# One order table for a whole kernel, weight loads per row chunk, 128-column kv weights and early query tiles

## The chip, the cores and the metric

The kernel runs on one core of one Trainium2 chip. The metric is the device time of one execution in microseconds; lower is better. A profile is one further view: it counts from the first to the last instruction, which is about 1.7 us less than the device time of the same execution. "PE" is TensorE, "DVE" VectorE, "ACT" ScalarE, "POOL" GpSimd, "SP" the engine that issues most DMAs, "PEld" the weight loads of PE.

## The reference

```python
# S=2048 tokens, D=640, H=32 heads of 20, F=1728; all bf16
x = A_x
g = sigmoid((x * gate_w).sum(-1, keepdims=True))
# a: linear attention
q, k, v = split_heads(x @ wqkv)                      # 2048 x 640 each
pq, pk = q @ w_phi, k @ w_phi                        # per head, 20 x 20
phi = lambda p: concat([softmax(p), softmax(-p)])    # 40 features a head
kv = einsum("bhsf,bhsd->bhfd", phi(pk), v)           # sums over all tokens
z  = phi(pk).sum(tokens)
a  = (phi(pq) @ kv) / (phi(pq) . z + 1e-6) @ wo
# b: gated FFN
b = (silu(x @ w_gate) * (x @ w_up)) @ w_down
return g * a + (1 - g) * b
```

## The kernel before

The program is straight-line: Python functions emit instructions, and a tracker puts semaphore waits between them. Work is cut into items: the transposes of a token tile of x (`xpose`), its values (`vtile`), its keys (`ktile`), its kv sums (`kvtile`), its queries (`qtile`), a gate-and-up item of the FFN (`fitem`: 10 matmuls of 512 columns), an attention output (`oitem`), a down projection (`ditem`). The order in which the items are emitted is the order on every engine. Before, that order came from numbers: each item was given a position on an axis, and the list was sorted.

```python
put(-20, xpose, 0); put(-20, gcol); put(-19, vhalf, 0, 0); put(-18.5, xpose, 1); ...
for m in range(5):
    put(-10 + 0.1 * m, premult, 1, m)                       # keys: wk times w_phi
    put((2.1, 3.1, 3.3, 3.4, 4.4)[m], premult, 0, m)        # queries: wq times w_phi
for t in range(NT):                                         # 16 token tiles of 128
    put(t, ktile, t); put(t + 3.6, kvtile, t)
    if t >= 6: put(t - 2.2, vtile, t)
put(NT + 2.7, kv_finish); put(NT + 4.2, z_broadcast)
...                                                         # fitem, qtile, oitem, ditem
```

The kv sums, and the query tile, whose VectorE work was emitted in two parts, one and two items after the exponentials:

```python
def kvtile(t):
    for j in range(NCH):                                    # 11 blocks of 3 heads x 40 features
        o = bank(bk, 63 * jj, 63 * jj + 63, 0, 120)
        pairs.append((o, ekr[:, b, 120 * j:120 * j + 120],  # weights: 120 columns
                      v1r[:, t % NV, 63 * j:63 * j + 63], ...))

def qtile(t):
    pr = tok_proj(t, 0); head_exps(pr, e)                   # PE, then two exponentials on ACT
    def vec_a():
        reduce(qz, e); tt("dve", ez, e, zb, mult)           # sums, numerators of the denominator
    def vec_b():
        reduce(qw, ez); ...                                 # small operations, then the scaling
        tt("pool", ph, eq, qc, mult); dma(phiT, ph, transpose=True)
    defer(1, vec_a); defer(2, vec_b)
```

The softmax here doesn't subtract the row's maximum and nothing guards it: scores larger than these inputs give would overflow.

Of the kernel before, what the change touches and what calls it, by code (L numbers as in the profile page):

```python
# [18 lines left out]
ACTF = mybir.ActivationFunctionType
# [5 lines left out]
BANK = 2048  # L25

# [144 lines left out]
def _build(nc, A_x, A_wqkv, A_w_phi, A_wo, B_x, B_w_gate, B_w_up, B_w_down, gate_w, out):  # L171
# [37 lines left out]
    qz = sb("qz", [P, 2, 64], F32)  # L209
# [7 lines left out]
    ekr = nc.alloc_sbuf_tensor_at("ekr", [P, 4, FP], BF16, offset=hbase + 14 * 512 * 2)  # L217
# [93 lines left out]
    def memset(e, a, v):  # L311
        eo = tr.eng[e]
        return run(e, lambda: eo.memset(a, v), [], [a])

    def dma(e, dst, src, transpose=False):
        eo = tr.eng[e]

        def fn():
            if transpose:
                return eo.dma_start_transpose(dst, src)  # L320
            return eo.dma_start(dst, src)
        rd = [src] if src.tensor.name in tr.base else []
        wr = [dst] if dst.tensor.name in tr.base else []
        return run(e, fn, rd, wr, dma=True)
# [16 lines left out]
    wv_src = A_wqkv[:, 2 * D:3 * D].rearrange("(c p) j -> p c j", p=P)  # L341
    wk_src = A_wqkv[:, D:2 * D].rearrange("(c p) j -> p c j", p=P)
# [3 lines left out]
    dma("sp", wvg[:, :, 0:320], wv_src[:, :, 0:320])  # L346
    load_x(1)
    dma("sp", wvg[:, :, 320:D], wv_src[:, :, 320:D])
    load_x(2)
    load_x(3)  # L350
    dma("sp", wkn[:, :, :], wk_src)
# [21 lines left out]
    v1v = v1r[:, :, :].rearrange("p b (h d) -> p b h d", d=DH + 1)  # L373
    memset("dve", v1v[:, :, H, :], 0.0)
    memset("dve", v1v[:, :, :, DH:DH + 1], 1.0)
    memset("dve", ekr[:, :, 1280:FP], 0.0)
    memset("dve", krec[:, :, :], 0.0)
    memset("pool", wog[:, :, :], 0.0)
    memset("pool", ones[:, :], 1.0)
# [24 lines left out]
    deferred = []  # L404

    def tick():
        for d in deferred:
            d[0] -= 1
        while deferred and deferred[0][0] <= 0:
            deferred.pop(0)[1]()  # L410

    def defer(n, fn):
        deferred.append([n, fn])
        deferred.sort(key=lambda d: d[0])

    ring = {"n": 3, "i": 0}
# [19 lines left out]
    vpr = {}  # L436

    def vhalf(t, hb):
        if t not in vpr:
            vpr[t] = next_pair()  # L440
        pr = vpr[t]
        n = 320 + hb
        mm(group(bank(2 * pr + hb, 0, n), [(xT[:, t, c, :], wvg[:, c, 320 * hb:320 * hb + n]) for c in range(5)]))
        if hb:
            i = halves(pr).rearrange("p b (h d) -> p b h d", d=DH)
            o = v1v[:, t % NV, 0:H, 0:DH].rearrange("p (b h) d -> p b h d", b=2)
            copy("act", o, i)
            copy("act", svec[:, t:t + 1], bank(2 * pr + 1, 320, 321))

    def vtile(t):  # L450
        vhalf(t, 0)
        vhalf(t, 1)
# [31 lines left out]
    def kvtile(t):  # L484
        b = t % 4
        pairs = []
        for j in range(NCH):
            bk, jj = (KV0, j) if j < 8 else (KV0 + 1, j - 8)
            o = bank(bk, 63 * jj, 63 * jj + 63, 0, 120)
            pairs.append((o, ekr[:, b, 120 * j:120 * j + 120], v1r[:, t % NV, 63 * j:63 * j + 63],  # L490
                          t == 0 and jj == 0, t == NT - 1, True))
        mm(pairs)
# [56 lines left out]
    def swapped(t, b):  # L549
        return bass.AP(t, 64 * b + 1, [[128, P], [2, 32], [-1, 2]])  # L550

    def qtile(t):
        pr = tok_proj(t, 0)
        b = t % 3
        s = t % 2
        e = eq[:, b, 0:1280]
        head_exps(pr, e)

        def vec_a():
            reduce(qz[:, s, :], e.rearrange("p (g d) -> p g d", d=DH))  # L560
            tt("dve", ez[:, s, :], e, zb[:, 0:1280], ALU.mult)

        def vec_b():
            reduce(qw[:, s, :], ez[:, s, :].rearrange("p (g d) -> p g d", d=DH))
            stt(qw[:, s, :], qz[:, s, :], 0.5e-6, qw[:, s, :], ALU.mult, ALU.add)
            qs = swapped(qz, s)
            v2 = lambda a: a.rearrange("p (h s) -> p h s", s=2)
            run("dve", lambda: dve.tensor_tensor(v2(qm[:, s, :]), v2(qw[:, s, :]), qs, ALU.mult),  # L568
                [qw[:, s, :], qz[:, s, :]], [qm[:, s, :]])
            m2 = v2(qm[:, s, :])  # L570
            tt("dve", qd[:, s, :], m2[:, :, 0], m2[:, :, 1], ALU.add)
            recip(qd[:, s, :], qd[:, s, :])
            run("dve", lambda: dve.scalar_tensor_tensor(  # L573
                out=v2(qc[:, s, 0:64]), in0=qs, scalar=g2[:, t:t + 1],
                in1=qd[:, s, :].unsqueeze(2).to_broadcast([P, 32, 2]), op0=ALU.mult, op1=ALU.mult),
                [qz[:, s, :], qd[:, s, :], g2[:, t:t + 1]], [qc[:, s, 0:64]])
            f = ph[:, b, :].rearrange("p (j c) -> p j c", c=P)[:, :, 0:120]
            tt("pool", f.rearrange("p j (g d) -> p j g d", d=DH),
               eq[:, b, :].rearrange("p (j g d) -> p j g d", j=NCH, d=DH),
               qc[:, s, :].rearrange("p (j g) -> p j g", j=NCH).unsqueeze(3).to_broadcast([P, NCH, 6, DH]),  # L580
               ALU.mult)
            dma("sp", phiT[:, (t // 4) % 2, t % 4, :, :], ph[:, b, :], transpose=True)
        defer(1, vec_a)
        defer(2, vec_b)

# [49 lines left out]
    def ditem(bt, u):  # L635
        buf = bt % 2
        t = 4 * bt + u
        pr = next_pair()
        tok = slice(P * u, P * u + P)
        ls = [(hT[:, buf, k, tok], wd[:, k, :]) for k in range(13)]  # L640
        ls += [(hT[0:104, buf, 13, tok], wd[0:104, 13, :])]
        ls += [(oT[:, buf, m, tok], wog[:, m, :]) for m in range(5)]
        pairs = []
        n = len(ls)
        for i, (l, r) in enumerate(ls):
            for hb in range(2):
                pairs.append((bank(2 * pr + hb, 0, 320), l, r[:, 320 * hb:320 * hb + 320],
                              i == 0, i == n - 1, False))
        mm(pairs)
        o = osb[:, t % 4, :]  # L650
        actop(o.rearrange("p (b c) -> p b c", b=2), halves(pr), ACTF.Copy, omg[:, t:t + 1])
        out_evs.append(dma("sp", out2[t * P:(t + 1) * P, :], o))


    def item(fn, *a):
        fn(*a)
        tick()

    def widen():
        ring["n"] = 4  # L660

    todo = []

    def put(pos, fn, *a):
        todo.append((pos, len(todo), fn, a))

    def ring3():
        ring["n"] = 3


    ring["n"] = 4
    put(-20, xpose, 0)
    put(-20, gcol)
    put(-19, vhalf, 0, 0)
    put(-18.5, xpose, 1)
    put(-18, vhalf, 0, 1)
    put(-17.5, xpose, 2)
    put(-17.4, xpose, 3)
    put(-17, vhalf, 1, 0)
    put(-17, vhalf, 1, 1)  # L680
    put(-15, vtile, 2)
    put(-14, vtile, 3)
    for m in range(5):
        put(-13 + 0.1 * m, wxpose, m)
        put(-10 + 0.1 * m, premult, 1, m)
        put((2.1, 3.1, 3.3, 3.4, 4.4)[m], premult, 0, m)
    put(-13.5, xpose, 4)
    put(-11, vtile, 4)
    put(-11.1, xpose, 5)
    put(3.5, ring3)  # L690
    put(-7, load_ffn_weights)
    put(-9.55, vtile, 5)
    for t in range(NT):
        put(t, ktile, t)
        put(t + 3.6, kvtile, t)
        if t >= 6:
            put(t - 2.2, vtile, t)
    put(NT - 0.5, gates)
    put(NT + 2.7, kv_finish)
    put(NT + 2.71, tail_weights)  # L700
    put(NT + 4.2, z_broadcast)
    put(NT + 4.2, widen)
    S0 = NT - 0.3
    SL = 17.0
    for i in range(14):
        put(S0 + 0.65 * i, fitem, 0, i)
# [67 lines left out]
```

## Time and profile before

| | before |
|---|---|
| median device time, 3 runs | 308.45 us |
| profiled execution | 306.99 us, span 305.3, granted clock 1.000 |
| PE busy | 291.9 us (96%) |
| first matmul / last matmul ends / span ends | 3.18 / 302.3 / 305.26 us |

The first part of the page before: busy time, share of the span and instruction count of each engine.

```profile
PE 291.9 (96%) x1967; PEld 178.2 (58%) x1967; DVE 163.7 (54%) x249; ACT 149.4 (49%) x251; POOL 156.5 (51%) x121
```

PE is the engine to look at; every other one is near half. The view of waits tells who held PE up: total, number of times, longest.

```profile
PE ps L267 <- DVE hT L299: 4.3, 4, 2.6
PE ps L279 <- DMA xs<-in_A_x_dram: 3.2, 1, 3.2
PE ps L267 <- DMA wvg<-in_A_wqkv_dram: 1.4, 1, 1.4
PE ps L267 <- ACT ekr L285: 0.8, 1, 0.8
PE ps L267 <- ACT wqk L285: 0.5, 1, 0.5
```

These are only 10 of some 16 us that can be lost, because a "busy" PE is not always at its pace (below, 258 ns for a matmul of 320 columns near 6 us, 136 ns later). What I use for that throughout is a **lag**: the start of a matmul minus the time that all matmuls before it take at their undisturbed start-to-start distance in these traces (216 ns for 512 columns, 136 for 320, 56 for 128, 55 for a kv matmul with 120-column weights, small groups at their own median; warm-ups count nothing). It is worked out from the timeline. If the lag grows between two points, time was lost there, by a wait or by a slow clock.

| lag (us) at | before | after |
|---|---|---|
| first key tile | 7.90 (at 20.73 us) | 8.55 (at 18.65) |
| last kv sum | 9.23 | 8.58 |
| first attention output | 10.71 | 8.65 |
| first FFN item after it | 13.82 | 8.94 |
| end of the matmuls | 16.37 | 10.83 |

Two groups of weight loads by form before: shapes are array rows*columns, then elements; behind the bar busy time and mean ns of one, then idle time of the engine before them.

```profile
L267 PEld LDWEIGHTS ps<-v1r,ekr 128*120 128x120 bf16 x176 | 12.0, 135 | 2.0 <-ACT ekr L285 1.0
L267 PEld LDWEIGHTS ps<-wqk,xT 128*128 128x128 bf16 x320 | 31.0, 98 | 14.9 <-ACT hT L285 0.4 <-ACT us L285 0.4
```

The kv weights, with 120 columns, are the only group near full size that takes 135 ns and not 98 at full pace (the transposes of x average 130, because 20 of their 30 loads lie in the first 10 us, most at about 150 ns; the other 10 take 94 to 98). The timeline of PE in the first 10 us shows the start (start, duration, what, count, wait before):

```profile
3.18 0.72 PE L279 MATMUL ps<-ident,xs 128*128 128x128 bf16 x5 [3.18 <-DMA xs<-in_A_x_dram]
...
5.41 1.49 PE L267 MATMUL ps<-wvg,xT 128*128 128x320 bf16 x5 [1.40 <-DMA wvg<-in_A_wqkv_dram]
6.70 0.74 PE L279 MATMUL ps<-ident,xs 128*128 128x128 bf16 x5
```

From 5.41 to 6.70 lie five matmuls of 320 columns: 258 ns each, about half the later pace. The half pace ends at 10.28 us. The profile's record of the granted clock has no entry before that time and reads full clock from there, so the mean clock of a run does not count the start; that the half pace of the start is a half clock is inferred from the like factor in e2 below (427 ns against 216, beside a recorded half clock).

Last, the timeline of DVE before around the largest loss, at the first attention output:

```profile
126.72 1.28 DVE L299 SCALAR_TENSOR_TENSOR hT<-hT,ps 128x512 bf16<-128x512 bf16 x2
127.92 1.48 DVE L306 TENSOR_REDUCE qz<-eq 128x64 f32<-128x1280 bf16 x1
129.32 1.79 DVE L295 TENSOR_TENSOR ez<-eq,zb 128x1280 bf16<-128x1280 bf16 x1
131.03 0.68 DVE L299 SCALAR_TENSOR_TENSOR hT<-hT,ps 128x512 bf16<-128x512 bf16 x1
```

PE waits until 131.76 for a PSUM pair. The evacuation that frees it (131.03) stands behind 3.1 us of query work on DVE (127.92 to 131.03), emitted ahead of it; in this view each record starts within 0.1 us of the end of the one before.

### The profile page before, as it was taken

What the parts mean: (1) busy time and instruction counts of PE and PEld (TensorE: products, weight loads), DVE (VectorE), ACT (ScalarE), POOL (GpSimd) and SP (SyncE); (2) the same over time, 40 slices, a digit from 0 to 9 for tenths busy, and PEclk for the clock granted to TensorE, in tenths of its full rate; (3) what the DMA queues carried; (4) which work ended last, traced back from release to release, by engine and by line L of the source; (5) the groups of instructions that cost most, each with busy time, mean ns of one, the idle gap of its engine ahead of it and who ended that gap; (6) DMA issues with size and microseconds to landing.
All of it is one profiled execution on the core that took longest, in us unless ns stands there. A gap on an engine that the chain in (4) does not pass through costs nothing.

```text
span 305.3 us, 4854 instructions
## 1 busy us (share of the span) xinstructions
PE 291.9 (96%) x1967; PEld 178.2 (58%) x1967; DVE 163.7 (54%) x249; ACT 149.4 (49%) x251; POOL 156.5 (51%) x121
## 2 busy tenths in 40 slices
PE   3998999999999999879999999999999999999996
PEld 2776777775445544346666446646645555556774
DVE  1258466588647899961616656647157372811000
ACT  1449666664475766634243582343277354436111
POOL 5905866778745588882323574361525536443000
PEclk9999999999999999999999999999999999999999
DMA  8977995200000222223030220330202203030101
GB/s 227 234 122 142 365 360 151 55 3 1 0 2 0 47 49 47 47 47 71 21 71 21 48 44 5 70 71 9 62 21 47 43 28 69 3 69 0 45 21 43
DMA packets 45319, 21.25 MB, mean 70 GB/s; under 512 B 34354, under 2 KB 45298, under 8 KB 45298
## 3 DMA queue, kind: packets, MB, share of 16 engines
q1 hardware_dynamic: 44632, 20.93, 27.6%
q8 instruction: 15, 0.25, 0.4%
q10 hardware_dynamic: 666, 0.03, 0.2%
q14 instruction: 6, 0.05, 0.1%
HBM read 10.10 MB, written 2.62 MB: 42 GB/s over the span
## 4 chain that ended last, share of the span: by engine, by line
PE 77%; DVE 16%; ACT 4%; DMA 1%; issue 1%; SPq 0%
PE ps L267 76%; DVE hT L299 3%; DVE qz L306 3%; DVE qw L306 3%; DVE ez L295 3%; ACT ekr L285 2%; ACT eq L285 1%; DMA wvg<-in_A_wqkv_dram 1%; PE ps L279 1%; DVE dz L295 1%; DVE qd L309 1%; ACT wqk L285 1%; DVE qc L573 1%; DVE qw L299 0%; DVE qm L568 0%
## 5 line engine op out<-in xcount | busy, mean ns | idle before, releaser
L295 POOL TENSOR_TENSOR hT<-hT,us 128x512 bf16<-128x512 bf16 (+1 forms) x56 | 66.4, 1195 | 60.1 <-DVE hT L299 60.1
L299 DVE SCALAR_TENSOR_TENSOR hT<-hT,ps 128x512 bf16<-128x512 bf16 (+1 forms) x56 | 37.7, 682 | 63.4 <-ACT hT L285 52.2
L267 PE MATMUL ps<-xT,wg 128*128 128x512 bf16 x260 | 64.6, 379 | 3.1 <-DVE hT L299 3.1
L267 PE MATMUL ps<-xT,wu 128*128 128x512 bf16 x260 | 64.6, 379 | 0.0
L267 PE MATMUL ps<-wd,hT 128*128 128x320 bf16 x448 | 63.5, 299 | 0.0
L285 ACT ACTIVATE hT<-ps 128x512 bf16<-128x512 f32 (+2 forms) x60 | 35.8, 596 | 54.3 <-PE ps L267 54.1
L295 POOL TENSOR_TENSOR ph<-eq,qc 128x1320 bf16<-128x1320 bf16 x16 | 38.8, 2425 | 40.9 <-DVE qc L573 30.3
L267 PEld LDWEIGHTS ps<-wd,hT 128*128 128x128 bf16 x448 | 43.8, 98 | 18.3
L267 PE MATMUL ps<-wqk,xT 128*128 128x320 bf16 x320 | 48.4, 299 | 0.0
L295 POOL TENSOR_TENSOR ekr<-ekr,krec 128x1280 bf16<-128x1280 bf16 x16 | 37.5, 2357 | 20.0 <-DVE krec L309 20.0
L285 ACT ACTIVATE osb<-ps,omg 128x640 bf16<-128x640 f32 x16 | 12.7, 793 | 63.5 <-PE ps L267 63.5
L267 PEld LDWEIGHTS ps<-xT,wu 128*128 128x128 bf16 x260 | 25.4, 98 | 30.7
L267 PEld LDWEIGHTS ps<-xT,wg 128*128 128x128 bf16 x260 | 24.9, 98 | 30.1 <-DVE hT L299 3.5
L267 PEld LDWEIGHTS ps<-wqk,xT 128*128 128x128 bf16 x320 | 31.0, 98 | 14.9 <-ACT hT L285 0.4
L306 DVE TENSOR_REDUCE qz<-eq 128x64 f32<-128x1280 bf16 x16 | 23.7, 1483 | 19.1 <-ACT eq L285 19.1
L285 ACT ACTIVATE us<-ps 128x512 bf16<-128x512 f32 (+1 forms) x56 | 33.2, 592 | 0.7 <-POOL hT L295 0.6
L306 DVE TENSOR_REDUCE ksum<-ekr 128x64 f32<-128x1280 bf16 x16 | 23.5, 1468 | 17.2 <-ACT ekr L285 17.2
L267 PE MATMUL ps<-wvg,xT 128*128 128x320 bf16 (+1 forms) x160 | 25.9, 312 | 1.9 <-DMA wvg<-in_A_wqkv_dram 1.4
L285 ACT ACTIVATE ekr<-ps 128x640 bf16<-128x640 f32 x32 | 22.4, 703 | 8.0 <-PE ps L267 7.5
L285 ACT ACTIVATE eq<-ps 128x640 bf16<-128x640 f32 x32 | 22.5, 703 | 3.9 <-PE ps L267 3.3
L267 PE MATMUL ps<-wog,oT 128*128 128x320 bf16 x160 | 24.3, 299 | 0.0
L306 DVE TENSOR_REDUCE qw<-ez 128x64 f32<-128x1280 bf16 x16 | 23.7, 1479 | 0.1
(68 smaller groups left out, 196.2 us busy)
## 6 DMA issues: line engine op xcount, KB each, us to landing
out_dram<-osb SPq DMA_DIRECT2D x16, 160.0 KB, 1.8
wd<-in_B_w_down_dram SPq DMA_DIRECT2D x1, 2080.0 KB, 15.7
xs<-in_A_x_dram SPq DMA_DIRECT2D x6, 160.0 KB, 4.6
wvg<-in_A_wqkv_dram SPq DMA_DIRECT2D x2, 400.0 KB, 4.3
wkn<-in_A_wqkv_dram SPq DMA_DIRECT2D x1, 800.0 KB, 6.3
wg<-in_B_w_gate_dram SPq DMA_DIRECT2D x1, 800.0 KB, 9.2
wu<-in_B_w_up_dram SPq DMA_DIRECT2D x1, 800.0 KB, 10.9
wog<-in_A_wo_dram SPq DMA_DIRECT2D x2, 375.0 KB, 6.6
```

Source lines behind the costliest of these rows:

```text
L267: last = pe.matmul(o, lhsT=l, rhs=r, start=st, stop=sp_, skip_group_check=sk)
L279: last = pe.transpose(o, i, ident[0:k, 0:k])
L285: return run("act", lambda: act.activation(o, i, func, scale=scale), rd, [o])
L295: return run(e, lambda: eo.tensor_tensor(o, a, b, op), [a, b], [o])
L299: return run("dve", lambda: dve.scalar_tensor_tensor(out=o, in0=a, scalar=s, in1=b, op0=op0, op1=op1), rd, [o])
L306: return run("dve", lambda: dve.tensor_reduce(o, i, AX.X, ALU.add), [i], [o])
L309: return run("dve", lambda: dve.reciprocal(o, i), [i], [o])
L573: run("dve", lambda: dve.scalar_tensor_tensor(out=v2(qc[:, s, 0:64]), in0=qs, scalar=g2[:, t:t + 1], in1=qd[:, s, :].unsqueeze(2).to_broad ...
```

## The change

Its intent: emit everything from one written table, with the query tile cut into three VectorE parts that can be placed one by one; start as soon as the first rows of the weights are there, with dummy matmuls ahead of them to end the half pace (10.28 us above) sooner; use weights of 128 columns for the kv sums; and run three query tiles among the last keys. The core of the diff:

```diff
+ORDER = """
+L H X0 X1 G V0 X2 V1 X3 W1 V2 W3 W2 M1 W4 W0 X5 M3 M2 M0 M4 V3 X4 K0 K1 V4 V5 I K2 K3 E0 V6 K4 E1
+V7 R3 E2 K5 R0 K6 E3 V8 K7 E4 R2 V9 K8 R1 E5 V10 V11 K9 E6 V12 K10 E7 V13 E8 R4 K11 K12 E9 K13
+E10 Q0 V14 K14 V15 A0 E11 K15 E12 F0.0 Q1 J E13 F0.1 E14 Q2 E15 N F0.2 A1 F0.3 A2 F0.4 Z T F0.5
+B0 C0 F0.6 F0.7 F0.8 B1 F0.9 B2 F1.0 C1 Q3 F0.10 C2 A3 Q4 F1.1 B3 F0.11 C3 Q5 F1.2 A4 A5 F1.3 Q6
+F0.12 B4 F1.4 F1.5 O0.0 O0.1 A6 C4 O0.2 B5 F1.6 ... D3.3          (cut: 4 more lines)
+"""
+    ops = {"H": warm, "X": xpose, "V": vtile, "W": wxpose, "M": premult keys, "R": premult queries,
+           "K": ktile, "E": kvtile, "N": kv_end, "Z": z_broadcast, "Q": qtile (PE and ACT),
+           "A": qsum, "B": qden, "C": qscale, "F": fitem, "O": oitem, "D": ditem, ...}
+    for w in ORDER.split(): ops[w[0]](*...)

-    dma("sp", wvg[:, :, 0:320], wv_src[:, :, 0:320])       # by column halves, all 5 chunks each
-    load_x(1)
-    dma("sp", wvg[:, :, 320:D], wv_src[:, :, 320:D])
+    for c in range(5):
+        load_rows(wvg[:, c, 0:D], c, 2 * D)                # by row chunks, 1280 B a row
+        if c == 1: load_x(1)
 ...
+    def warm():
+        pr = next_pair()
+        mm([(bank(2 * pr, 0, P), ones[:, :], ones[:, :], True, True, False)] * NWARM)   # 12

-            o = bank(bk, 63 * jj, 63 * jj + 63, 0, 120)
-            pairs.append((o, ekr[:, b, 120 * j:120 * j + 120], ...
+            o = bank(bk, 63 * jj, 63 * jj + 63)
+            pairs.append((o, ekr[:, b, 120 * j:120 * j + P], ...      # 8 columns of the next block, unused

-        defer(1, vec_a)          # reduce qz, ez
-        defer(2, vec_b)          # reduce qw, ..., POOL, DMA
+    def qsum(t): reduce(qz ...)
+    def qden(t): tt("dve", ez, eq, zb, mult)
+    def qscale(t): reduce(qw ...); ...; tt("pool", ...); dma(...)
```

The last output tile is also computed, evacuated and stored by column halves.

More of the change, by code (lines that the diff above doesn't have):

```diff
@@ L17 @@
 NV = 6
+NWARM = 12
 FP = 120 * NCH
+FK = FP + 8
 ACTF = mybir.ActivationFunctionType
@@ L25 @@
 BANK = 2048
+ORDER = """
[3 more added lines that the diff above has]
+B0 C0 F0.6 F0.7 F0.8 B1 F0.9 B2 F1.0 C1 Q3 F0.10 C2 A3 Q4 F1.1 B3 F0.11 C3 Q5 F1.2 A4 A5 F1.3 Q6
+F0.12 B4 F1.4 F1.5 O0.0 O0.1 A6 C4 O0.2 B5 F1.6 F1.7 F1.8 F0.13 Q7 F1.9 C5 Q8 A7 F1.10 D0.0 F1.11
+B6 B7 C6 D0.1 D0.2 Q9 C7 A8 A9 D0.3 O1.0 F2.0 Q10 B8 F1.12 B9 O1.1 O1.2 F1.13 F2.1 C8 A10 C9 F2.2
+Q11 F2.3 D1.0 F2.4 A11 B10 C10 F2.5 F2.6 B11 F2.7 F2.8 Q12 Q13 A12 C11 F2.9 A13 B12 F2.10 D1.1
+B13 D1.2 F2.11 Q14 C12 F2.12 D1.3 F3.0 O2.0 A14 F3.1 B14 F2.13 Q15 O2.1 C13 A15 F3.2 O2.2 C14 B15
+F3.3 C15 F3.4 D2.0 F3.5 D2.1 F3.6 O3.0 O3.1 F3.7 F3.8 F3.9 F3.10 O3.2 D2.2 F3.11 F3.12 F3.13 D2.3
+D3.0 D3.1 D3.2 D3.3
+"""
 class _Tracker:
@@ L208, in _build @@
     ph = sb("ph", [P, 3, NCH * P], BF16)
-    qz = sb("qz", [P, 2, 64], F32)
+    qz = sb("qz", [P, 3, 64], F32)
     qw = sb("qw", [P, 2, 64], F32)
@@ L216, in _build @@
     hbase = nc.lookup_mloc(hT).addr
-    ekr = nc.alloc_sbuf_tensor_at("ekr", [P, 4, FP], BF16, offset=hbase + 14 * 512 * 2)
+    ekr = nc.alloc_sbuf_tensor_at("ekr", [P, 4, FK], BF16, offset=hbase + 14 * 512 * 2)
     tr.reg(ekr, "sbuf", hbase + 14 * 512 * 2)
@@ L339, in load_x, with load_rows @@
             dma("sp", xT[:, t, :, :], x2[t * P:(t + 1) * P, :], transpose=True)
-    wv_src = A_wqkv[:, 2 * D:3 * D].rearrange("(c p) j -> p c j", p=P)
-    wk_src = A_wqkv[:, D:2 * D].rearrange("(c p) j -> p c j", p=P)
+    def load_rows(dst, c, c0):
+        dma("sp", dst, A_wqkv[c * P:(c + 1) * P, c0:c0 + D])
     dma("act", gwr[0:5, :], bass.AP(gate_w.tensor, gate_w.offset, [[P, 5], [1, P]]))
@@ L345, in _build @@
     load_x(0)
-    dma("sp", wvg[:, :, 0:320], wv_src[:, :, 0:320])
-    load_x(1)
-    dma("sp", wvg[:, :, 320:D], wv_src[:, :, 320:D])
+    for c in range(5):
+        load_rows(wvg[:, c, 0:D], c, 2 * D)
+        if c == 1:
+            load_x(1)
     load_x(2)
     load_x(3)
-    dma("sp", wkn[:, :, :], wk_src)
+    for c in range(5):
+        load_rows(wkn[:, c, :], c, D)
     for t in range(4, 7):
@@ L373, in _build @@
     v1v = v1r[:, :, :].rearrange("p b (h d) -> p b h d", d=DH + 1)
+    memset("dve", ones[:, :], 1.0)
     memset("dve", v1v[:, :, H, :], 0.0)
     memset("dve", v1v[:, :, :, DH:DH + 1], 1.0)
-    memset("dve", ekr[:, :, 1280:FP], 0.0)
+    memset("dve", ekr[:, :, 1280:FK], 0.0)
     memset("dve", krec[:, :, :], 0.0)
     memset("pool", wog[:, :, :], 0.0)
-    memset("pool", ones[:, :], 1.0)
     memset("pool", kvsb[:, :, :], 0.0)
@@ L401, in tail_weights @@
         copy("pool", wt[:, :, 64:P], wu[:, :, 13 * P:F_FFN])
-    deferred = []
-    def tick():
-        for d in deferred:
-            d[0] -= 1
-        while deferred and deferred[0][0] <= 0:
-            deferred.pop(0)[1]()
-    def defer(n, fn):
-        deferred.append([n, fn])
-        deferred.sort(key=lambda d: d[0])
-    ring = {"n": 3, "i": 0}
+    ring = {"n": 4, "i": 0}
     def next_pair():
@@ L434, in gcol @@
         copy("dve", wvg[:, :, D:D + 1], o.unsqueeze(2))
-    vpr = {}
-    def vhalf(t, hb):
-        if t not in vpr:
-            vpr[t] = next_pair()
-        pr = vpr[t]
-        n = 320 + hb
-        mm(group(bank(2 * pr + hb, 0, n), [(xT[:, t, c, :], wvg[:, c, 320 * hb:320 * hb + n]) for c in range(5)]))
-        if hb:
-            i = halves(pr).rearrange("p b (h d) -> p b h d", d=DH)
-            o = v1v[:, t % NV, 0:H, 0:DH].rearrange("p (b h) d -> p b h d", b=2)
-            copy("act", o, i)
-            copy("act", svec[:, t:t + 1], bank(2 * pr + 1, 320, 321))
-    def vtile(t):
-        vhalf(t, 0)
-        vhalf(t, 1)
+    def warm():
+        pr = next_pair()
+        mm([(bank(2 * pr, 0, P), ones[:, :], ones[:, :], True, True, False)] * NWARM)
+    def vtile(t):
+        pr = next_pair()
+        pairs = [(bank(2 * pr + hb, 0, 320 + hb), xT[:, t, c, :], wvg[:, c, 320 * hb:640 + hb - 320 * (1 - hb)],
+                  c == 0, c == 4, False) for c in range(5) for hb in range(2)]
+        if t == 0:
+            for c in range(5):
+                mm(pairs[2 * c:2 * c + 2])
+        else:
+            mm(pairs)
+        i = halves(pr).rearrange("p b (h d) -> p b h d", d=DH)
+        o = v1v[:, t % NV, 0:H, 0:DH].rearrange("p (b h) d -> p b h d", b=2)
+        copy("act", o, i)
+        copy("act", svec[:, t:t + 1], bank(2 * pr + 1, 320, 321))
     def head_exps(pr, dst):
@@ L488, in kvtile @@
             bk, jj = (KV0, j) if j < 8 else (KV0 + 1, j - 8)
-            o = bank(bk, 63 * jj, 63 * jj + 63, 0, 120)
-            pairs.append((o, ekr[:, b, 120 * j:120 * j + 120], v1r[:, t % NV, 63 * j:63 * j + 63],
+            o = bank(bk, 63 * jj, 63 * jj + 63)
+            pairs.append((o, ekr[:, b, 120 * j:120 * j + P], v1r[:, t % NV, 63 * j:63 * j + 63],
                           t == 0 and jj == 0, t == NT - 1, True))
@@ L549, in swapped @@
     def swapped(t, b):
-        return bass.AP(t, 64 * b + 1, [[128, P], [2, 32], [-1, 2]])
+        return bass.AP(t, 64 * b + 1, [[192, P], [2, 32], [-1, 2]])
     def qtile(t):
@@ L557, in qtile @@
         head_exps(pr, e)
-        def vec_a():
-            reduce(qz[:, s, :], e.rearrange("p (g d) -> p g d", d=DH))
-            tt("dve", ez[:, s, :], e, zb[:, 0:1280], ALU.mult)
-        def vec_b():
-            reduce(qw[:, s, :], ez[:, s, :].rearrange("p (g d) -> p g d", d=DH))
-            stt(qw[:, s, :], qz[:, s, :], 0.5e-6, qw[:, s, :], ALU.mult, ALU.add)
-            qs = swapped(qz, s)
-            v2 = lambda a: a.rearrange("p (h s) -> p h s", s=2)
-            run("dve", lambda: dve.tensor_tensor(v2(qm[:, s, :]), v2(qw[:, s, :]), qs, ALU.mult),
-                [qw[:, s, :], qz[:, s, :]], [qm[:, s, :]])
-            m2 = v2(qm[:, s, :])
-            tt("dve", qd[:, s, :], m2[:, :, 0], m2[:, :, 1], ALU.add)
-            recip(qd[:, s, :], qd[:, s, :])
-            run("dve", lambda: dve.scalar_tensor_tensor(
-                out=v2(qc[:, s, 0:64]), in0=qs, scalar=g2[:, t:t + 1],
-                in1=qd[:, s, :].unsqueeze(2).to_broadcast([P, 32, 2]), op0=ALU.mult, op1=ALU.mult),
-                [qz[:, s, :], qd[:, s, :], g2[:, t:t + 1]], [qc[:, s, 0:64]])
-            f = ph[:, b, :].rearrange("p (j c) -> p j c", c=P)[:, :, 0:120]
-            tt("pool", f.rearrange("p j (g d) -> p j g d", d=DH),
-               eq[:, b, :].rearrange("p (j g d) -> p j g d", j=NCH, d=DH),
-               qc[:, s, :].rearrange("p (j g) -> p j g", j=NCH).unsqueeze(3).to_broadcast([P, NCH, 6, DH]),
-               ALU.mult)
-            dma("sp", phiT[:, (t // 4) % 2, t % 4, :, :], ph[:, b, :], transpose=True)
@@ L583, in qtile, with qsum, qden, qscale @@
-        defer(1, vec_a)
-        defer(2, vec_b)
+    def qsum(t):
+        e = eq[:, t % 3, 0:1280]
+        reduce(qz[:, t % 3, :], e.rearrange("p (g d) -> p g d", d=DH))
+    def qden(t):
+        tt("dve", ez[:, t % 2, :], eq[:, t % 3, 0:1280], zb[:, 0:1280], ALU.mult)
+    def qscale(t):
+        b = t % 3
+        s = t % 2
+        reduce(qw[:, s, :], ez[:, s, :].rearrange("p (g d) -> p g d", d=DH))
+        stt(qw[:, s, :], qz[:, b, :], 0.5e-6, qw[:, s, :], ALU.mult, ALU.add)
+        qs = swapped(qz, b)
+        v2 = lambda a: a.rearrange("p (h s) -> p h s", s=2)
+        run("dve", lambda: dve.tensor_tensor(v2(qm[:, s, :]), v2(qw[:, s, :]), qs, ALU.mult),
+            [qw[:, s, :], qz[:, b, :]], [qm[:, s, :]])
+        m2 = v2(qm[:, s, :])
+        tt("dve", qd[:, s, :], m2[:, :, 0], m2[:, :, 1], ALU.add)
+        recip(qd[:, s, :], qd[:, s, :])
+        run("dve", lambda: dve.scalar_tensor_tensor(
+            out=v2(qc[:, s, 0:64]), in0=qs, scalar=g2[:, t:t + 1],
+            in1=qd[:, s, :].unsqueeze(2).to_broadcast([P, 32, 2]), op0=ALU.mult, op1=ALU.mult),
+            [qz[:, b, :], qd[:, s, :], g2[:, t:t + 1]], [qc[:, s, 0:64]])
+        f = ph[:, b, :].rearrange("p (j c) -> p j c", c=P)[:, :, 0:120]
+        tt("pool", f.rearrange("p j (g d) -> p j g d", d=DH),
+           eq[:, b, :].rearrange("p (j g d) -> p j g d", j=NCH, d=DH),
+           qc[:, s, :].rearrange("p (j g) -> p j g", j=NCH).unsqueeze(3).to_broadcast([P, NCH, 6, DH]),
+           ALU.mult)
+        dma("sp", phiT[:, (t // 4) % 2, t % 4, :, :], ph[:, b, :], transpose=True)
@@ L642, in ditem @@
         ls += [(oT[:, buf, m, tok], wog[:, m, :]) for m in range(5)]
-        pairs = []
         n = len(ls)
-        for i, (l, r) in enumerate(ls):
-            for hb in range(2):
-                pairs.append((bank(2 * pr + hb, 0, 320), l, r[:, 320 * hb:320 * hb + 320],
-                              i == 0, i == n - 1, False))
-        mm(pairs)
-        o = osb[:, t % 4, :]
-        actop(o.rearrange("p (b c) -> p b c", b=2), halves(pr), ACTF.Copy, omg[:, t:t + 1])
-        out_evs.append(dma("sp", out2[t * P:(t + 1) * P, :], o))
@@ L655, in item @@
-    def item(fn, *a):
-        fn(*a)
-        tick()
-    def widen():
-        ring["n"] = 4
-    todo = []
-    def put(pos, fn, *a):
-        todo.append((pos, len(todo), fn, a))
-    def ring3():
-        ring["n"] = 3
-    ring["n"] = 4
-    put(-20, xpose, 0)
-    put(-20, gcol)
-    put(-19, vhalf, 0, 0)
-    put(-18.5, xpose, 1)
-    put(-18, vhalf, 0, 1)
-    put(-17.5, xpose, 2)
-    put(-17.4, xpose, 3)
-    put(-17, vhalf, 1, 0)
-    put(-17, vhalf, 1, 1)
-    put(-15, vtile, 2)
-    put(-14, vtile, 3)
@@ L683, in _build @@
-    for m in range(5):
-        put(-13 + 0.1 * m, wxpose, m)
-        put(-10 + 0.1 * m, premult, 1, m)
-        put((2.1, 3.1, 3.3, 3.4, 4.4)[m], premult, 0, m)
-    put(-13.5, xpose, 4)
-    put(-11, vtile, 4)
-    put(-11.1, xpose, 5)
-    put(3.5, ring3)
-    put(-7, load_ffn_weights)
-    put(-9.55, vtile, 5)
-    for t in range(NT):
-        put(t, ktile, t)
-        put(t + 3.6, kvtile, t)
-        if t >= 6:
-            put(t - 2.2, vtile, t)
-    put(NT - 0.5, gates)
-    put(NT + 2.7, kv_finish)
@@ L700, in _build @@
-    put(NT + 2.71, tail_weights)
-    put(NT + 4.2, z_broadcast)
-    put(NT + 4.2, widen)
-    S0 = NT - 0.3
-    SL = 17.0
-    for i in range(14):
-        put(S0 + 0.65 * i, fitem, 0, i)
-    S1 = S0 + 0.65 * 14
-    for t in range(NT):
-        put(NT + 4.4 + 2.7 * t if t < 4 else S1 + 6.2 + 3.4 * (t - 4), qtile, t)
-    for s in range(1, NB + 1):
-        a = S1 + SL * (s - 1)
-        if s < NB:
-            for i in range(14):
-                put(a + SL * (i + 0.5) / 14, fitem, s, i)
-        o0, d0, dd = {1: (10.8, 12, 1.5), 2: (5.2, 7, 3.1), 3: (1.7, 4, 4.4), 4: (-1.3, 2, 4)}[s]
-        for p in range(3):
-            put(a + o0 + 0.3 * p, oitem, s - 1, p)
-        for u in range(4):
-            put(a + d0 + dd * u, ditem, s - 1, u)
@@ L720, in _build @@
-    todo.sort(key=lambda z: z[:2])
-    for _, _, fn, a in todo:
-        item(fn, *a)
-    while deferred:
-        tick()
+        half = [[(bank(2 * pr + hb, 0, 320), l, r[:, 320 * hb:320 * hb + 320], i == 0, i == n - 1, False)
+                 for i, (l, r) in enumerate(ls)] for hb in range(2)]
+        o = osb[:, t % 4, :]
+        if t < NT - 1:
+            mm([p for ab in zip(*half) for p in ab])
+            actop(o.rearrange("p (b c) -> p b c", b=2), halves(pr), ACTF.Copy, omg[:, t:t + 1])
+            out_evs.append(dma("sp", out2[t * P:(t + 1) * P, :], o))
+            return
@@ new lines, in ditem, with kv_begin, kv_end @@
+        for hb in range(2):
+            mm(half[hb])
+            c = slice(320 * hb, 320 * hb + 320)
+            actop(o[:, c], bank(2 * pr + hb, 0, 320), ACTF.Copy, omg[:, t:t + 1])
+            out_evs.append(dma("sp", out2[t * P:(t + 1) * P, c], o[:, c]))
+    def kv_begin():
+        ring["n"] = 3
+    def kv_end():
+        kv_finish()
+        ring["n"] = 4
+    ops = {
+        "H": warm, "X": xpose, "G": gcol, "V": vtile, "W": wxpose,
+        "M": lambda m: premult(1, m), "R": lambda m: premult(0, m),
+        "K": ktile, "E": kvtile, "L": load_ffn_weights, "T": tail_weights, "J": gates,
+        "I": kv_begin, "N": kv_end, "Z": z_broadcast,
+        "Q": qtile, "A": qsum, "B": qden, "C": qscale,
+        "F": fitem, "O": oitem, "D": ditem,
+    }
@@ L725, in _build @@
+    for w in ORDER.split():
+        ops[w[0]](*[int(a) for a in w[1:].split(".") if a])
     for s, v in out_evs:
```

## The prediction

> **What bounds it now.** TensorE. The page's busy list gives PE 291.9 of 305.3 us (96%); the chain that ended last is 77% PE, 16% DVE. Start-to-start distances in the timeline show PE's undisturbed pace: 216 ns per 512-column matmul, 136 per 320-column, 35 per 80-column, 55 per 63-column kv matmul. Counts times paces give 285.8 us (estimate). The last matmul ends at 302.3, so 16.5 us are lost before it: 3.2 ahead of the first matmul, 4.7 more by 20 us (267 ns per 320 columns until about 10 us; a 1.4 us wait for the first values weights), 1.7 at 27-30 us (PE behind ACT, which runs the q premultiply copies in a burst), 4.1 at 126-132 us (waits view: PE behind DVE, 4.3 in all; DVE is 97% busy from 100 to 130), about 2.5 in small waits at 84, 178, 231 and 275. A tail of 3.0 us (ACT 0.79, then the output DMA) follows.
>
> **What changes, costed.**
> 1. kv sums with 128-column weights. The groups by form show 135 ns per weight load of 120 columns, 98 for every one of 128; kv matmuls stream only 63 columns yet start 55 ns apart, while 80-column matmuls with 128-column weights start 35 apart. So the load sets the pace. [...] Expect about 30 ns: 176 x 25 = -4.5 us, all critical: in the key phase PE then needs about 3.0 us per token tile, POOL 2.4, ACT 2.3, DVE 1.9.
> 2. Start: row-chunk loads (1280 B rows instead of 640) let tile 0's values begin with the first chunk; 12 warm-up matmuls run while PE only waits. [...] More DMA issues (about 0.45 us each) push the transposing loads some 2.7 us later; I expect slack for that. Lag at the first key tile 7.9 -> about 6: -1.9 us.
> 3. q premultiplies spread among keys: -1.4 of 1.7 us.
> 4. Three query tiles among the keys, their first reduction (1.48 us) early, more FFN items before the first attention output: the 4.1 us nearly vanish: -3.8. Smaller waits: -1.3.
> 5. Last output tile by halves: ACT 0.79 -> about 0.45, a smaller last DMA: -0.5 us.
> Added: nothing heavy; DVE, ACT and POOL do the same work.
>
> Sum -13.4; I keep +0.4 for new small waits. Predicted **295.5 us**, 8 in 10 within 292.5 to 299.5. Faster by over 2%: 0.95; within 2%: 0.045; slower: 0.005.
>
> **What would show it.** Step 1: kv weight loads of about 98 ns, kv matmuls about 30 ns apart, PE busy down 4 us or more. Step 2: first real matmul still near 3.2 us, tile 0's values from about 4.5 us, 136 ns pace before 9 us, first key tile 2 us earlier. Steps 3, 4: in the waits view PE behind DVE and ACT under 1 us; no PE gap over 1 us after 20 us; DVE below 95% between 100 and 130 us. Step 5: last matmul to span end about 2.5 us.
>
> **What would make it wrong.** kv matmuls staying near 55 ns: +4.5. The start bound by landing of the weights rather than by clock: up to +2. The faster key phase becoming bound by POOL or ACT (three query tiles add 4.2 us of ACT there): +1 to 3. Vector work pulled forward colliding with the kv finishing on DVE.

4.5 + 1.9 + 1.4 + 3.8 + 1.3 + 0.5 is the 13.4. The 30 ns of step 1 are the estimate from the 35 ns at 80 columns. In step 2, that warm-up matmuls would shorten the half pace was an assumption, which no trace had shown.

## More of the kernel before

PSUM is used as a ring of pairs of banks: each item takes the next pair. While the kv sums accumulate in the fourth pair, the ring has three pairs, otherwise four.

## The result

| | before | after |
|---|---|---|
| median device time, 4 runs each | 308.41 us (308.2 to 308.54) | 297.0 us (296.87 to 297.67) |
| ratio after/before | | 0.9635, 95% interval 0.9619 to 0.9652 |
| profiled span | 305.3 us | 295.2 us |

A ratio is the mean time of one kernel's fast runs over that of the other's of the same rounds, so it is not quite the ratio of the medians.

The page and the waits of PE after, to be set beside those of before:

```profile
PE 288.2 (98%) x1979; PEld 174.3 (59%) x1979; DVE 168.1 (57%) x250; ACT 148.4 (50%) x252; POOL 160.1 (54%) x120
```

```profile
PE ps L296 <- DMA xs<-in_A_x_dram: 2.9, 2, 2.2
PE ps L284 <- DVE ones L330: 1.1, 1, 1.1
PE ps L284 <- DVE wvg L308: 0.6, 1, 0.6
```

Every wait that is left lies in the first 8 us; the waits behind DVE's evacuations and behind ACT are gone. The chain that ended last is 97% PE. The weight loads of the kv group after:

```profile
L284 PEld LDWEIGHTS ps<-v1r,ekr 128*128 128x128 bf16 x176 | 7.6, 98 | 1.2
```

Start to start, the 176 matmuls that use them went from 56.3 to 31.4 ns in the mean: 9.9 -> 5.5 us in all. The start did not get better, as the timeline of PE after shows:

```profile
1.13 1.46 PE L284 MATMUL ps<-ones 128*128 128x128 bf16 x12 [1.13 <-DVE ones L330]
3.23 0.71 PE L296 MATMUL ps<-ident,xs 128*128 128x128 bf16 x5 [0.64 <-DMA xs<-in_A_x_dram]
6.16 0.72 PE L296 MATMUL ps<-ident,xs 128*128 128x128 bf16 x5 [2.22 <-DMA xs<-in_A_x_dram]
...
7.54 2.82 PE L284 MATMUL ps<-wvg,xT 128*128 128x320 bf16 x10 [0.56 <-DVE wvg L308]
10.20 0.45 PE L296 MATMUL ps<-ident,xs 128*128 128x128 bf16 x5
```

The table puts tile 1's transposes (X1) and the gate column (G) ahead of tile 0's values (V0). Tile 1 of x is now issued behind two weight chunks and holds PE until 6.16. So V0 begins at 7.54, against 5.41 before, and still at half pace: 10 matmuls in 2.66 us. The half pace ends at 10.2 us (10.28 before); the 12 warm-ups, which end at 2.6 us, were followed by waits of 0.64 and 2.22 us. One profile does not fix this start: the lag at the first key tile was 8.2 to 10.0 us in the seven profiles that share it (after, e1, e5, e8 to e11), and 7.90 and 8.21 us in the two with the old start (before, e2).

Where the 10.1 us between the two profiles came from (lags above, and after, at 32 ns for a kv matmul with 128-column weights, 8.55 at 18.65 us, 8.58, 8.65, 8.94 and 10.83; pace of kv 55 -> 32 ns times 176):

| stage | us |
|---|---|
| kv matmuls at their undisturbed pace | -4.05 |
| start, up to the first key tile | +0.65 |
| keys, up to the last kv sum | -1.30 |
| kv finishing and first query tiles | -1.41 |
| the first attention output | -2.82 |
| the rest | -0.66 |
| last matmul to span end (2.96 -> 2.48) | -0.48 |

The medians differ by 11.4, which is 1.3 more. The profiled run of before was a lucky one: 306.99 us with a granted clock of 1.000. In the later groups the kernel before ran 21 more times, each with its mean clock noted: 2 runs at 1.000 (307.14 and 307.26 us), 15 at 0.993 to 0.994 (308.1 to 308.83) and 4 at 0.988 to 0.989 (309.65 to 310.09). The profile of a variant below (e2) shows what that can be: after the gap at the first attention output, PE's clock falls to half for 3.4 us. An estimate from that: one such drop lowers the mean clock of a run of 305 us by 0.0056 and two by 0.0112, close to the 0.994 and 0.989 noted. The changed kernel ran at 1.000 in all 8 of its runs (4 here, 4 as a control below); it has no PE gap over 1 us after 8 us. That the lower means of the kernel before come from this one place is inferred, since no profile of it caught the drop itself.

### The profile page after: what moved, and what is told of

Read it like the earlier page. It is cut to its first block, busy times and chain, and to the rows that moved or that the text cites. A ratio compares the mean times of both kernels' runs of the same rounds, so it can differ in the third digit from the quotient of the medians.

```text
span 295.2 us, 4901 instructions
## 1 busy us (share of the span) xinstructions
PE 288.2 (98%) x1979; PEld 174.3 (59%) x1979; DVE 168.1 (57%) x250; ACT 148.4 (50%) x252; POOL 160.1 (54%) x120
## 4 chain that ended last, share of the span: by engine, by line
PE 97%; DMA 1%; SPq 0%; DVE 0%; ACT 0%; issue 0%
PE ps L284 96%; DMA xs<-in_A_x_dram 1%; PE ps L296 1%; SPq L338 0%; ACT osb L302 0%; DVE xT L308 0%; DVE wvg L308 0%
## 5 line engine op out<-in xcount | busy, mean ns | idle before, releaser
L312 POOL TENSOR_TENSOR hT<-hT,us 128x512 bf16<-128x512 bf16 (+1 forms) x56 | 70.4, 1268 | 57.5 <-DVE hT L316 56.9
L312 POOL TENSOR_TENSOR ph<-eq,qc 128x1320 bf16<-128x1320 bf16 x16 | 39.8, 2489 | 31.7 <-DVE qc L587 31.7
L302 ACT ACTIVATE osb<-ps,omg 128x640 bf16<-128x640 f32 (+1 forms) x17 | 13.0, 763 | 58.9 <-PE ps L284 58.9
```

The lines of the kernel that those rows point to most:

```text
L302: return run("act", lambda: act.activation(o, i, func, scale=scale), rd, [o])
L312: return run(e, lambda: eo.tensor_tensor(o, a, b, op), [a, b], [o])
```

## The experiments

Twelve kernels ran, in three groups, each group on one chip. All gave correct results.

| run | edit | median us | ratio to before |
|---|---|---|---|
| e1_kv120 | after, kv weights of 120 columns | 301.19 | 0.9764 |
| e2_kv128_alone | before, kv weights of 128 columns | 306.50 | 0.9934 |
| e3_no_warm | after without the warm-up item | 303.45 | 0.9824 |
| e4_v0_first | after, V0 before X1 | 296.30 | 0.9609 |
| e5_after_again | after, control | 296.94 | 0.9623 |
| e6_no_warm_same_ring | after, warm-ups gone, ring turn kept | 297.25 | 0.9623 |
| e7_long_warm | after, 18 + 24 warm-ups | 294.93 | 0.9551 |
| e8_q_after_keys | after, query tiles 0 to 2 behind the keys | 298.95 | 0.9675 |
| e9_r_burst | after, q premultiplies in a burst | 301.87 | 0.9773 |
| e10_old_parts | after, query tiles 3 to 15 in the old two parts | 310.20 | 1.0045 |
| e11_kv124 | after, kv weights of 124 columns (one run) | 300.60 | |
| e12_warm_v0_first | e7, V0 before X1, loads reordered | 295.01 | 0.9553 |

### Is the weight load the pace of the kv sums?

e1, undoing that part:

```diff
-            o = bank(bk, 63 * jj, 63 * jj + 63)
-            pairs.append((o, ekr[:, b, 120 * j:120 * j + P], ...
+            o = bank(bk, 63 * jj, 63 * jj + 63, 0, 120)
+            pairs.append((o, ekr[:, b, 120 * j:120 * j + 120], ...
```

> The changed kernel with the kv sums back to 120-column weights, all else kept. Theory (the weight load sets the pace of these 176 matmuls, all on the critical path): start-to-start back from 31 to about 56 ns, weight loads back to 135 ns, time up by 4.4 us, 297.0 -> 301.4. Rival (in the changed order PE has slack there, so other engines hide it): up by under 1.5 us.

Measured: 0.9764 against the control's 0.9623, 1.4% or about 4.3 us. The matmuls were 55 ns apart in the median, the loads took 135 ns. Both are as the theory expects. e11 asks whether the step is at exactly 128 columns:

```diff
-            o = bank(bk, 63 * jj, 63 * jj + 63)
-            pairs.append((o, ekr[:, b, 120 * j:120 * j + P], ...
+            o = bank(bk, 63 * jj, 63 * jj + 63, 0, 124)
+            pairs.append((o, ekr[:, b, 120 * j:120 * j + 124], ...
```

> The changed kernel with kv weights of 124 columns instead of 128. Theory (there is a step at exactly 128 columns): loads of about 135 ns, matmuls about 57 ns apart, 4.4 us slower. Rival (the pace falls smoothly with the width, or 128 output rows matter in another way): about 33 to 45 ns apart.

The group of weight loads of e11, by form:

```profile
L284 PEld LDWEIGHTS ps<-v1r,ekr 128*124 128x124 bf16 x176 | 12.3, 137 | 0.7
```

Four columns fewer cost 39 ns a load; the matmuls were 57 ns apart, and the span was 298.9 us against the control's 294.9. There is a step between 124 columns and 128, and 124 is even a little slower than 120 (55 ns); 125 to 127 were not run. These edits change the number of output rows together with the width of the weights; that the load sets the pace, and not the rows, is inferred from the load's own time (135 and 137 ns against 98), not separated by a run. Filling up to 128 with 8 unused columns paid here: 32 ns a matmul against 55.

e2 does this part alone in the kernel before (with 8 more zeroed columns behind `ekr`):

```diff
-            o = bank(bk, 63 * jj, 63 * jj + 63, 0, 120)
-            pairs.append((o, ekr[:, b, 120 * j:120 * j + 120], ...
+            o = bank(bk, 63 * jj, 63 * jj + 63)
+            pairs.append((o, ekr[:, b, 120 * j:120 * j + P], ...
```

> The kernel before with 128-column kv weights as its only edit. Theory: 308.4 - 4.4 = 304.0 us, the matmuls 31 ns apart. Rival (the old order gives the freed time back in waits on ScalarE, VectorE or GpSimd): 306 us or more, with the waits of PE grown by as much.

Measured: 306.5 us, ratio 0.9934: about 2 us, half of what the same edit is worth in the changed order. The median distance was 32 ns, so the cause was removed; but the lag between first key tile and last kv sum grew by 2.76 us instead of 1.33. A new wait behind DVE at 72 us (0.95 us of lag) and a longer one behind ACT at 30 us (0.25 us more) took most of that back. The rival was nearer. In the old order, other engines' turns came due just when PE got faster; the new order is what makes the gain whole.

e2's profile also caught the clock drop. Its timeline of PE around the first attention output:

```profile
125.42 1.66 PE L267 MATMUL ps<-phiT,kvsb 120*64 120x512 bf16 x11 [0.78 <-DVE hT L299]
129.72 1.87 PE L267 MATMUL ps<-xT,wg 128*128 128x512 bf16 x5 [2.64 <-DVE hT L299]
131.38 2.34 PE L267 MATMUL ps<-xT,wu 128*128 128x512 bf16 x5
```

Behind the gap of 2.64 us, five matmuls from 131.38 take 2.13 us until the next instruction, 427 ns each where 216 is the pace. The profile's clock record has half clock from 130.2 to 133.6. The kernel before has nearly the same gap (2.65 us) in its profile without the drop.

### Are the warm-ups worth anything?

```diff
-L H X0 X1 G V0 X2 ...
+L X0 X1 G V0 X2 ...
```

> The changed kernel without the 12 warm-up matmuls. Theory (they end at 2.6 us, PE then idles most of 3.6 us, and the pace is cold until about 10 us anyway): no change, 297.0 +- 0.4, full pace still reached near 10 us. Rival (they bring the full pace forward): 0.7 to 2 us slower, 267 ns pace for longer.

This came out 6 us slower, which I had not expected under either theory. The timeline of PE in e3:

```profile
72.09 0.51 PE L284 MATMUL ps<-v1r,ekr 128*128 128x63 bf16 x11
76.31 2.31 PE L284 MATMUL ps<-xT,wg 128*128 128x512 bf16 x5 [3.71 <-DVE kvsb L312]
78.41 2.34 PE L284 MATMUL ps<-xT,wu 128*128 128x512 bf16 x5
```

The cause sits at 72 us, not at the start. The warm-up item also takes one turn of the PSUM ring. Without that turn, the first FFN item after the kv finishing lands on the very pair in which the kv sums lie and which DVE is still reading: 3.71 us of wait, then matmuls at half pace until 82.25 us, worth another 2.9 us. The clock record has half clock from 75.5 us, within the gap, to 82.3. The run confounded two things. e6 keeps the turn and drops only the matmuls:

```diff
     def warm():
         pr = next_pair()
+        return
         mm([(bank(2 * pr, 0, P), ones[:, :], ones[:, :], True, True, False)] * NWARM)
```

> The first run without warm-ups also took away the warm-up's turn in the ring of PSUM pairs, so that the first gate-and-up item after the kv finishing landed on the very pair that VectorE still read. Here the turn is kept and only the 12 matmuls go. Theory (the 6 us of that run came from the ring's turn and the clock drop after its 3.9 us gap, not from the warm-ups): within 0.6 us of the control, no PE gap near 72 us. Rival (the warm-ups themselves are worth it): 3 us or more slower than the control.

Measured: 297.25 us against 296.94 for the control, the same ratio 0.9623. The control:

> The changed kernel itself, as a control on the chip of this group. Both theories: about 297 us, granted clock at full rate from 10 to 13 us on without a drop.

The 12 warm-ups as they stand buy nothing that can be seen. A likely reason is the idle time behind them, which e7 fills; it also has more of them. It keeps the ring's turns.

```diff
-L H X0 X1 G V0 X2 ...
+L H0 X0 G H1 X1 V0 X2 ...
-    def warm():
-        pr = next_pair()
+    def warm(again):
+        pr = 0 if again else next_pair()
-        mm([...] * NWARM)
+        mm([...] * (24 if again else 18))
```

> The changed kernel with 18 warm-up matmuls first and 24 more after tile 0's transposes, so that PE does not idle while it waits for tile 1 of x; the ring's turns stay the same. Theory ([...]the 12 warm-ups fail because PE idles from 2.6 to 6.2 us): half pace ends between 5 and 8.5 us, tile 0's values run at 136 ns per matmul, first key tile 1.2 to 2.5 us earlier than the control's, time 1.2 to 3 us below it. Rival (dummy matmuls don't bring the clock up, or the landing of weights is the limit): within 0.6 us of the control.

Timeline of PE in e7:

```profile
1.12 2.10 PE L284 MATMUL ps<-ones 128*128 128x128 bf16 x18 [1.12 <-DVE ones L330]
...
3.97 2.74 PE L284 MATMUL ps<-ones 128*128 128x128 bf16 x24
6.50 0.74 PE L296 MATMUL ps<-ident,xs 128*128 128x128 bf16 x5
7.03 1.76 PE L284 MATMUL ps<-wvg,xT 128*128 128x320 bf16 x10
8.63 0.44 PE L296 MATMUL ps<-ident,xs 128*128 128x128 bf16 x5
```

PE never idles long, half pace ends at 7.3 us, and V0 takes 1.6 us instead of 2.66. The first key tile starts at 17.08 us, against 18.37 in the control. The time is 294.93 us, 2.0 below the control, and all four runs (294.69 to 295.36) lie below all of the control's (296.62 to 297.68). This version beats both kernels. How long it took to reach full pace differs: with 12 warm-ups, from the work that begins when tile 1 of x has landed (5.8 us in e11, 6.05 in e1, with one pause of 0.56 us in it) it took 4.0 us (e11) to 7.0 us (e1); with 42, it took 6.2 us from the first of them in e7 and 3.0 us in e12 below, whose first 18 are the same. So e7 has a gain in all its runs, but how soon full pace comes is not set by the number of warm-ups alone, and no run separates their number from the filling of the pause.

### Is the order at the start the limit?

```diff
-L H X0 X1 G V0 X2 ...
+L H X0 G V0 X1 X2 ...
```

> The changed kernel with token tile 1's transposes moved from before to after token tile 0's values. Theory (the start gained nothing because PE waits 2.2 us for tile 1 of x while the first weight chunks have landed): values of tile 0 start near 5 us instead of 7.5, first key tile 1.5 to 2.5 us earlier than 18.65, time 295 us. Rival (the start is bound by the landing of the weights themselves): first key tile under 0.7 us earlier, time 296.5 or more.

Measured: 296.3 us (295.78 to 297.25); its group held no control, but the ratio, 0.9609, is only 0.0014 below the later control's. V0 did start at 4.48, as expected, yet it waited 1 us for the third weight chunk and everything ran at half pace until 12.0 us. The key tile was not earlier (19.00 us). So in this profile my theory, that the wait for tile 1 costs the start, was not the whole: the clock ate what the order gained. But it is the profile of the slowest of the four runs, and the half pace ends as late as 12 or 13 us in some profiles of the unchanged start too; what the order is worth at the usual clock is not shown. e12 then does it with the clock up:

```diff
-L H0 X0 G H1 X1 V0 X2 ...
+L H0 X0 G H1 V0 X1 X2 ...
     for c in range(5):
         load_rows(wvg[:, c, 0:D], c, 2 * D)
-        if c == 1:
-            load_x(1)
+    load_x(1)
-    for c in range(5):
+    for c in (1, 3, 2, 4, 0):
         load_rows(wkn[:, c, :], c, D)
```

> The kernel of the long warm-up with tile 0's values ahead of tile 1's transposes, tile 1 of x loaded after all five weight chunks, and the key weights loaded in the order of their use. Theory (with the clock up, landing of the data is what is left at the start): values of tile 0 start about 0.5 us earlier, first key tile 0.4 to 1 us earlier than 17.08, time about 294.4. Rival (the later x tiles and key weights then arrive too late): no gain over 294.9, with a wait for a DMA in its place.

Measured: 295.01 us, ratio 0.9553; e7's was 0.9551. In the profile the first key tile came at 16.74, 0.34 us earlier than in e7. Half pace had ended at 4.2 us and tile 0's values began at 5.41, but the last three of them came 0.15 to 0.25 us apart and tile 2 of x then made PE wait 0.8 us. Over the runs nothing was gained. In this profile the landing of the data, after the clock, is the next limit.

### What ended the waits at the first attention output?

The prediction gave three reasons: early query tiles, their early reduction, and more FFN items ahead. The third is a plain error: counted in the two orders, 23 FFN items were emitted before the first attention output, and 19 are now. e8 moves the early query tiles back:

```diff
-E10 Q0 V14 K14 V15 A0 E11 K15 E12 F0.0 Q1 J E13 F0.1 E14 Q2 E15 N F0.2 A1 F0.3 A2 F0.4 Z T F0.5
-B0 C0 F0.6 F0.7 F0.8 B1 F0.9 B2 F1.0 C1 Q3 F0.10 C2 A3 Q4 ...
+E10 P V14 K14 V15 E11 K15 E12 F0.0 P J E13 F0.1 E14 P E15 N F0.2 F0.3 F0.4 Z T F0.5
+Q0 A0 F0.6 B0 F0.7 Q1 C0 A1 F0.8 B1 F0.9 Q2 C1 A2 F1.0 B2 F0.10 Q3 C2 A3 Q4 ...   (P: an empty ring turn)
```

> The changed kernel with query tiles 0 to 2 and their first reductions moved back behind the kv finishing; the ring's turns are kept by empty turns. Theory (early query tiles take load off VectorE where it is full, and that is what ends the waits at the first attention output): PE waits behind VectorE come back, 1.5 to 4 us, with a clock drop after a long gap, 299 to 303 us. Rival (the other rearrangements ended the waits): within 1 us of the control.

Measured: 298.95 us, 0.5% or 1.6 to 2.0 us slower than the control, at the lower edge of the expected 299 to 303 us, but not for the expected reason. The waits of PE in e8:

```profile
PE ps L296 <- DMA xs<-in_A_x_dram: 2.5, 2, 1.8
PE ps L284 <- DVE ones L330: 1.1, 1, 1.1
PE ps L284 <- POOL ekr L312: 0.8, 1, 0.8
PE ps L284 <- DVE wvg L308: 0.6, 1, 0.6
PE ps L284 <- DMA phiT<-ph: 0.2, 1, 0.2
```

No wait behind DVE's evacuations returned at the attention output. The new wait is behind POOL at 69 us: among the last keys the query tiles give PE something to do while POOL scales the keys. In the profile 1.25 us of lag arise after the first key tile; 1.2 more come from the start, where the half pace lasted to 12.25 us in this run. So the early query tiles fill a wait; they don't end the old one.

e10 puts query tiles 3 to 15 back into the old two parts and leaves everything else in its place:

```diff
-... Q3 F0.10 C2 A3 Q4 F1.1 B3 F0.11 C3 Q5 F1.2 A4 A5 F1.3 Q6 F0.12 B4 F1.4 F1.5 O0.0 O0.1 A6 C4 O0.2 ...
+... Q3 F0.10 A3 B3 C2 C3 Q4 F1.1 A4 B4 F0.11 C4 Q5 F1.2 A5 B5 F1.3 C5 Q6 F0.12 A6 B6 F1.4 C6 F1.5 O0.0 ...
```

> The changed kernel with query tiles 3 to 15 in the old two parts, first reduction with the multiply one item after the exponentials and the rest two items after; everything else in its place. Theory (it is the finer placing of VectorE's parts between the gate-and-up items that ended the 4.1 us of waits): PE waits behind VectorE of 1.5 to 4 us in all between 90 and 290 us, time 298.5 to 301. Rival (the early query tiles and the earlier attention output were enough): under 0.7 us of waits, under 1 us slower.

It is the slowest of all, 310.2 us, 0.4% slower than the kernel before. The waits of PE, and its timeline around the attention output:

```profile
PE ps L275 <- DVE hT L307: 9.7, 6, 2.6
```

```profile
108.19 1.25 PE L275 MATMUL ps<-xT,wg 128*128 128x512 bf16 x5 [2.53 <-DVE hT L307]
...
124.64 1.06 PE L275 MATMUL ps<-phiT,kvsb 120*64 120x512 bf16 x3 [2.56 <-DVE hT L307]
128.09 2.31 PE L275 MATMUL ps<-xT,wg 128*128 128x512 bf16 x5 [2.39 <-DVE hT L307]
```

The amount of work in the whole run is the same, and DVE was 97% busy from 100 to 110 us in e10 and in the changed kernel alike (9.65 and 9.72 of 10 us). What differs is what stands between two evacuations of FFN items in DVE's queue. Read from the timelines of DVE, as the time from the end of one evacuation to the start of the next: in e10, 9.1 us from 98.3 us on (two query tiles end up in a row), then 2.5 to 2.8 us ahead of every evacuation until 128 us, so that the backlog never shrinks. In the changed kernel, 5.4 us once at 97.9, then 1.1, 2.8, 2.7, 0.6, 0.7 and 0.7 us, and a piece of 4.9 us only at 116.6, when the attention output has begun: parts of query tiles 4 to 6, which the first attention output doesn't need, are held back until after it. In the kernel before, 2.5 to 3.1 us stood ahead of nearly every evacuation from 106.9 to 131 us. The timeline of DVE after, around the start of the attention output at 115.15 us, is to be set beside that of before; here DVE has caught up and waits for ACT:

```profile
111.88 0.68 DVE L316 SCALAR_TENSOR_TENSOR hT<-hT,ps 128x512 bf16<-128x512 bf16 x1
113.13 0.69 DVE L316 SCALAR_TENSOR_TENSOR hT<-hT,ps 128x512 bf16<-128x512 bf16 x1 [0.57 <-ACT hT L302]
113.73 0.82 DVE L312 TENSOR_TENSOR ez<-eq,zb 128x1280 bf16<-128x1280 bf16 x1
114.47 0.68 DVE L316 SCALAR_TENSOR_TENSOR hT<-hT,ps 128x512 bf16<-128x512 bf16 x1
115.89 0.69 DVE L316 SCALAR_TENSOR_TENSOR hT<-hT,ps 128x512 bf16<-128x512 bf16 x1 [0.74 <-ACT hT L302]
116.49 1.48 DVE L323 TENSOR_REDUCE qz<-eq 128x64 f32<-128x1280 bf16 x1
```

So the placing of the parts ended the waits, as the theory says. The size, 13 us, is not that of the change: this order was made for the finer parts, and putting coarse ones into it made that one place with two tiles in a row. The converse, the finer parts in the old order, was not run.

### Do spread premultiplies end the waits at 27 to 30 us?

```diff
-K0 K1 V4 V5 I K2 K3 E0 V6 K4 E1 V7 R3 E2 K5 R0 K6 E3 V8 K7 E4 R2 V9 K8 R1 E5 ... E8 R4 K11
+K0 K1 V4 V5 K2 R0 K3 R1 R2 R3 I E0 V6 K4 R4 E1 V7 E2 K5 K6 E3 V8 K7 E4 V9 K8 E5 ... E8 K11
```

> The changed kernel with the five q premultiplies back in a burst among key tiles 2 to 4, as before. Theory (spreading them ended the waits of PE behind ScalarE at 27 to 30 us): these waits come back, 1 to 1.7 us between 26 and 36 us, time up by about 1.4 us besides the start's own scatter of about 1 us. Rival (the two values tiles moved ahead of key tile 2 already give ScalarE the time): under 0.4 us of waits there.

Measured: 301.87 us, ratio 0.9773 against 0.9623, so 4.6 us. The timeline of PE in e9:

```profile
31.86 0.52 PE L284 MATMUL ps<-v1r,ekr 128*128 128x63 bf16 x11 [2.56 <-ACT wqk L302]
32.22 2.05 PE L284 MATMUL ps<-wvg,xT 128*128 128x320 bf16 x10
34.06 2.73 PE L284 MATMUL ps<-wqk,xT 128*128 128x320 bf16 x10
```

The wait behind ACT's copies of the premultiplied weights is back, 2.56 us, more than the 1.7 of before. Behind it, from 33.1 us, the clock drops: the 10 matmuls from 34.06 take 2.56 us instead of 1.36. Not every gap of that size had a drop behind it: after 2.53 us at 108 us in e10, and after 2.65 us at 131.76 in the profile of the kernel before, five matmuls of 512 columns took 1.09 us, the full pace. The theory holds; its size was short because the wait was longer than I expected and because I did not count the clock, 1.7 us of lag more.

## Why the prediction was right or wrong

It said 295.5 us, 292.5 to 299.5; it is 297.0. The sum was -13.4, the medians moved by 11.4, the profiles by 10.1.

1. **kv sums, -4.5.** Right in size, and as to the load as far as its own time shows (135 -> 98 ns; the rows were not separated): -4.4 from the sums of start-to-start distances (9.9 -> 5.5 us), shown by e1 and e11. That all of it lies on the critical path holds only in the new order; in the old one half is given back (e2). Its test "PE busy down 4 us or more" came out as 3.7, because the 12 warm-ups count as busy.
2. **The start, -1.9.** This is the step that failed. It counted on 1.9 us less lag at the first key tile; the lag became 0.65 us longer. I let V0 begin with the first chunk although the order I had before me puts X1 and G ahead of it; I took the warm-ups as useful, which no trace had shown, although PE idles behind them (e6: no difference). The test that I named, "first key tile 2 us earlier", was met (20.73 -> 18.65 us) and still wrong: 2.7 us of other matmuls had been moved behind that key tile. Only the lag shows this. My named risk, landing of the weights, was not the main one either; the half pace was (e7 ends it at 7.3 us and gains 2.0 us).
3. **Premultiplies, -1.4.** Right: -1.30 over the key stage, and e9 brings the wait back.
4. **Query tiles, -3.8, and smaller waits, -1.3.** Right in size: -4.2 over the stages from the last kv sum to the first FFN item after the attention output, -0.7 after. Wrong in reasons: not the early query tiles (e8) and not more FFN items, which became fewer, but where the parts stand between DVE's evacuations, and which are held back until after the attention output (e10). The early reductions were not tested alone. DVE was not under 95% everywhere either: 97% from 100 to 110 us, and yet no wait.
5. **Halves of the last tile, -0.5.** Right as far as the profiles show: the last evacuation takes 0.53 us instead of 0.79, and the tail went from 2.96 to 2.48 us. It was not tested alone.
6. **Not in the sum:** a clock drop, 1.3 us in most runs of the kernel before (inferred from their mean clocks, 0.994 and less), which its one profile did not show and which e2's profile has behind the old gap.

What stays open: why the half pace ends at 9.8 us in some runs and at 13 in others, and at 4.2 us in e12 but 7.3 in e7. No run here shows what sets it. Nor was the share of the row-chunk loads measured alone.

## What to carry to other kernels

Compare starts by work done, not by the clock: an item that starts earlier may only have less before it. When one engine is the limit, cut the work of the engine that frees its buffers into pieces and place each behind an evacuation; busy shares do not show this (DVE 97% from 100 to 110 us in e10 and in the changed kernel alike), the queue order does. Dummy matmuls helped here only where there were more of them and the real work followed without a pause (2.0 us in e7; nothing seen in e6 against e5). Gaps of 2.64 us (e2) and 2.56 us (e9) in PE were followed by 3.4 us at half clock, another 1.7 us each; gaps of 2.65 us (before) and 2.53 us (e10, at 108 us) were not. When an item is taken out for a test, keep the ring turns that it took.
